# Letting GpSimd make lower parts of weights and of chunk 2's q and k, and giving a planner the measured durations of joins and upper casts

## The chip, the core and the metric

The kernel runs on one core of one Trainium2 chip. Its engines are TensorE (PE, matmuls; PEld is its weight load), VectorE (DVE), ScalarE (ACT), GpSimd (POOL) and SyncE (SP, which issues most transfers). The metric is the time on the device of one execution, in microseconds, as the median of several runs; lower is better. In this kernel about 0.2% (1.2 us) is what such a measurement tells from no change.

## The reference

Attention with a sliding window and sink columns, then a two-layer network with a leaky activation:

```python
# q, k, v: batch 4, heads 8, length 768, head size 64; window 128, sinks 4
scores = scale * np.matmul(q, k.transpose(0, 1, 3, 2))
scores = np.where(is_sink | in_window, scores, -1e9)
a = np.exp(scores - max(scores)); a = a / (sum(a) + 1e-9)
x = np.matmul(a, v)                      # as 3072 x 512
h = x @ w_in                             # 512 x 2048
g = np.maximum(h, 0) + alpha * np.minimum(h, 0)
out = g @ w_out                          # 2048 x 512
```

All inputs are float32 but the weights, which arrive as float64.

## The kernel before

**Tiling.** The 3072 rows are 12 chunks of 256 rows (c = 0 to 11, three for each batch). The 2048 hidden columns are 16 blocks of 128 (f = 0 to 15); block f holds 128 columns of w_in and 128 rows of w_out, as two halves of 512 columns each (half 0 is w_in's, half 1 w_out's). Every product of the network is made of three matmuls in a 19-bit format, high x high, high x low and low x high, where the lower part of a number is the number less its rounded upper part.

**Weights.** `convert_weights` (line 425) turns block f from float64 to these two parts in four steps over 1024 columns: an upper cast (line 436, on DVE or ACT) into the tile `zeros`, a join (line 441, DVE) into the tile `joined`, the high part (line 454, mostly ACT) and the low part (line 457, DVE, one subtraction over both halves). `zeros` and `joined` exist once, so the join of the next block waits for the low part of this one. All 16 blocks are converted between 7 and 106 us; `gemm1` (line 987) needs half 0 of a block, `gemm2` (lines 1043 to 1046) half 1.

**Attention.** From chunk 2 on, for each of 8 heads, `prep_head` (line 618) makes the high parts of k and q on ACT (lines 629, 630) and their low parts on DVE (lines 631, 633); `unit` (line 639) makes a score tile on PE (lines 668, 669) in one of two PSUM banks "s"; `soften` (line 676) adds the mask and takes the row minimum on DVE (line 683), which frees the bank, and the exponential on ACT (line 689); `finish_head` (line 693) makes 1/sum on DVE (lines 720, 721), the weighted window on DVE (line 732) and the sink columns on POOL (line 736).

**Network.** For each chunk and block, 12 matmuls of `gemm1`, the activation in three steps (ACT 996, DVE 998, ACT 1002), its low part (line 1005, on DVE, or on POOL for chunks below `ALONE`), and 6 matmuls of `gemm2`. Two neighbouring chunks may share a block: then the 12 matmuls of `gemm1` move 512 columns instead of twice 12 that move 256. `SHARED` says how many blocks chunk c shares with chunk c + 1.

**Order.** A planner (`Plan`, line 92) gets every operation with an engine, a cost in us, what it reads and writes, and for some an `other` engine with its own cost. `draw` (line 168) places them in order of time on each engine, by rank, and an operation goes to its other engine where it could start over 0.3 us sooner there. Operations with `locks` on DVE and on POOL are placed so that no two of them overlap: while one of them runs on POOL, DVE is given only operations without that mark. The order so found is fixed for each engine's queue; at run time, an engine waits at the head of its queue for what the operation needs. So a wrong cost changes no result, but puts an operation ahead of others that would have been ready.

Of the kernel before, what the change touches and what calls it, by code (L numbers as in the profile page):

```python
# [50 lines left out]
OVER = 1  # L51
# [7 lines left out]
AHEAD = 4  # L59
HALVED = 0  # L60
BUSY = 6
ALONE = 3
FIRST = 4
SHARED = {3: 3, 4: min(5, 6), **{c: 6 for c in range(5, 11)}}
EXP_LOW = 2.0 ** -15
EXP_HIGH = 122880.0
WIDEST = 2.0 ** 100
# [288 lines left out]
def program(ctx, tc, qk, pairs, vp, vq, vs, w, par, out):  # L356
# [68 lines left out]
    def convert_weights(f):  # L425
        raw, fin, first = raws[f], Block(None), None
        fins[f] = fin
        parts = ((0,), (1,)) if f < HALVED else ((0, 1),)
        for halves in parts:
            n = len(halves) * DM  # L430
            cols = slice(halves[0] * DM, halves[0] * DM + n)
            keys = lambda v, halves=halves: [(v, i) for i in halves]

            def upper(engine, cols=cols):
                to = zeros.at[:, cols].bitcast(F16).rearrange("p (x s) -> p x s", s=2)[:, :, 1]
                (nc.scalar.copy if engine == "ACT" else nc.vector.tensor_copy)(to, raw.at[:, cols].bitcast(BF16).rearrange("p x (w s) -> p x w s", s=2)[:, :, 1, 0])
            ways = [("DVE", 0.03 + 0.73e-3 * n, lambda upper=upper: upper("DVE")), ("ACT", 0.1 + 1.1e-3 * n, lambda upper=upper: upper("ACT"))]
            mine = ways.pop(f >= BUSY)
            o = op(*mine, reads=keys(raw), writes=keys(zeros), other=ways[0], locks=True)
            first = first or o  # L440
            op("DVE", 0.06 + 1.19e-3 * n, lambda cols=cols: nc.vector.scalar_tensor_tensor(
                joined.at[:, cols], raw.at[:, cols, 0], 13, zeros.at[:, cols], op0=ALU.logical_shift_right, op1=ALU.bitwise_or),
               reads=keys(raw) + keys(zeros), writes=keys(joined), locks=True)
        for halves in parts:
            a, b = halves[0], halves[-1] + 1
            keys = lambda v, halves=halves: [(v, i) for i in halves]
            n = (b - a) * DM
            wf = lambda a=a, b=b: joined.at.bitcast(F32).rearrange("p (i x) -> p i x", i=2)[:, a:b]

            def high_part(engine, a=a, b=b, wf=wf):  # L450
                if fin.at is None:
                    fin.tile = const.tile([P, 2, 2, DM], F32R, tag=f"w{f}", name=f"w{f}")
                    fin.at = [fin.tile[:, i] for i in range(2)]
                (nc.scalar.copy if engine == "ACT" else nc.vector.tensor_copy)(fin.tile[:, a:b, 0], wf())
            op("ACT", cast(n), lambda high_part=high_part: high_part("ACT"), reads=keys(joined), writes=[(fin, (i, 0)) for i in halves] + ([raw] if a == 0 else []),
               other=("DVE", dve(n, True), lambda high_part=high_part: high_part("DVE")))
            op("DVE", dve(n), lambda a=a, b=b, wf=wf: nc.vector.tensor_tensor(
                fin.tile[:, a:b, 1], wf(), fin.tile[:, a:b, 0].bitcast(F32), ALU.subtract),
               reads=keys(joined) + [(fin, (i, 0)) for i in halves], writes=[(fin, (i, 1)) for i in halves], locks=True)
        return first  # L460

    def weigh(f):
# [155 lines left out]
    def prep_head(c, h):  # L618
        st = stage.pop((c, h))
        if c in SPLIT:  # L620
            r = slice(h % 2 * D, (h % 2 + 1) * D)
            prep[c, h] = (st, r)
            return
        kq = val("kq")
        qh, ql = [lambda s=s: kq.at[:, s] for s in (slice(2 * KG, 2 * KG + QC), slice(2 * KG + QC, 2 * KG + 2 * QC))]
        n = 0 if c % CPB else P
        ks = lambda: kq.at[:, :2 * KG].rearrange("p (y x) -> p y x", y=2)[:, :, :KX]
        q_raw, k_raw = lambda: st.at[:, KC:], lambda: st.at[:, :KC].rearrange("p (y x) -> p y x", y=2)[:, :, n // 2:]
        op("ACT", cast(KC - n), lambda: nc.scalar.copy(ks()[:, :, n // 2:], k_raw()), reads=[st], writes=[(kq, "k")])  # L629
        op("ACT", cast(QC), lambda: nc.scalar.copy(qh(), q_raw()), reads=[st], writes=[(kq, "q")])  # L630
        op("DVE", dve(KC - n), lambda: nc.vector.tensor_tensor(ks()[D:, :, n // 2:], k_raw()[D:], ks()[D:, :, n // 2:].bitcast(F32), ALU.subtract),  # L631
           reads=[st], writes=[(kq, "k")], locks=True)
        op("DVE", dve(QC), lambda: nc.vector.tensor_tensor(ql(), q_raw(), qh().bitcast(F32), ALU.subtract),
           reads=[st, (kq, "q")], writes=[(kq, "l")], locks=True)
        prep[c, h] = (kq, qh, ql, ks)

    softened = []
# [55 lines left out]
    def finish_head(c, h):  # L693
        pt, nm, sm = ptile_.pop((c, h)), nms[c], sums[c]
        sk = sink[c]
        if h == H - 1:
            op("DVE", 0.1, lambda: nc.vector.tensor_tensor(fm, fm, nm.at.rearrange("p h u -> p (h u)"), ALU.max),
               reads=[nm], writes=[known("fm")])
        if c in SPLIT:
            op("POOL", 0.17, lambda: nc.gpsimd.tensor_copy(sk.at[:, :, h], pt.at[:, :, P:P + NS]), reads=[pt], writes=[(sk, h)])  # L700
            tp = bank(c, h, "pa")
            for u in range(2):
                o = 2 * u * P
                both = u > 0 or c % CPB > 0

                def turn(u=u, o=o, both=both):
                    if both:
                        nc.tensor.transpose(tp.at[:, o:o + P], pt.at[:, u, 0:P], ident)
                    nc.tensor.transpose(tp.at[:, o + P:o + 2 * P], pt.at[:, u, P + NS:], ident)
                op("PE", (1 + both) * TURN, turn, reads=[(pt, u), known("ident")], writes=[tp], tail=T_TAIL)  # L710
            o = P if c % CPB == 0 else 0
            lends = c == 0 and h >= 4
            t = val("v" if lends else "comb")
            turned_ = (lambda: t.at.rearrange("p a h d -> p (a h d)")) if lends else (lambda: t.at[:, o:])
            op("ACT", cast(4 * P - o, True), lambda: nc.scalar.copy(turned_(), tp.at[:, o:]), reads=[tp], writes=[t],
               other=("DVE", dve(4 * P - o), lambda: nc.vector.tensor_copy(turned_(), tp.at[:, o:])) if c == 0 else None)
            wt.setdefault((c, h // 2), []).append((t, lambda cols: turned_()[:, cols.start - o:cols.stop - o]))
            return
        ri = val("ri")
        op("DVE", 0.15, lambda: nc.vector.tensor_scalar(ri.at[:, :2], sm.at[:, h], 1e-9, None, op0=ALU.add), reads=[(sm, (h, 0)), (sm, (h, 1))], writes=[ri], locks=True)  # L720
        op("DVE", 0.08, lambda: nc.vector.reciprocal(ri.at[:, :2], ri.at[:, :2]), writes=[ri])  # L721
        if h % 2 == 0:
            comb[c, h // 2] = val("comb")
        cb = comb[c, h // 2]
        view = lambda: cb.at.rearrange("p (j u x) -> p j u x", j=2, u=2)[:, h % 2]
        for u in range(2):
            if u == 0 and c % CPB == 0:
                op("DVE", 0.2, lambda: nc.vector.tensor_scalar(view()[:, 0], pt.at[:, 0, P + NS:], ri.at[:, 0:1], None, op0=ALU.mult),
                   reads=[(pt, 0), ri], writes=[(cb, (h % 2, 0))], locks=True)
                continue  # L730
            jk = val("jk")
            op("DVE", 0.28, lambda u=u, jk=jk: nc.vector.tensor_tensor_reduce(  # L732
                out=view()[:, u], in0=pt.at[:, u, 0:P], in1=pt.at[:, u, P + NS:], scale=ri.at[:, u:u + 1], scalar=0.0,
                op0=ALU.add, op1=ALU.max, accum_out=jk.at[:, u:u + 1]),
                reads=[(pt, u), ri], writes=[(cb, (h % 2, u)), jk])
        op("POOL", 0.2, lambda: nc.gpsimd.tensor_tensor(  # L736
            sk.at[:, :, h], pt.at[:, :, P:P + NS], ri.at[:, :2].unsqueeze(2).broadcast_to([P, 2, NS]), ALU.mult),
            reads=[pt, ri], writes=[(sk, h)])
        if c >= PAIRED and h % 2:
            swap(c, h // 2)  # L740
# [425 lines left out]
    groups += [[(0, f), (1, f)] for f in range(LEAD, NF)]  # L1166
    groups += [[(1, f), (1, f + 1)] for f in range(FORE, LEAD, 2)]
    work = [[] for _ in range(2 * NF)]
    for at_, steps in ((0, spread(attention(1), OVER)), (2 * NF - LATE, spread([st for some in attention(2) for st in some or [None]] + [None] * 4, LATE))):
        for n, todo in enumerate(steps):  # L1170
            work[at_ + n] += todo
    pend = []
# [262 lines left out]
```

## Time and profile before

| | |
|---|---|
| median of three runs | 619.73 us (619.46 to 619.85) |
| the profiled execution | 619.43 us, of which span 617.6 us |
| PE / PEld busy | 609.1 us (99%) / 541.2 us (88%) |
| DVE / ACT / POOL busy | 484.2 (78%) / 379.4 (61%) / 44.6 us (7%) |
| granted TensorE clock, mean | 0.999 |

A row of a timeline is: start, duration, engine, line, operation, output and inputs, shapes, count, and in brackets how long the engine had been idle before and what ended that. A matmul's duration is that from its first column to its last result; the next one may start before it ends. Line numbers are those of the kernel before.

### The profile page before, as it was taken

What the parts mean: (1) busy time and instruction counts of PE and PEld (TensorE: products, weight loads), DVE (VectorE), ACT (ScalarE), POOL (GpSimd) and SP (SyncE); (2) the same over time, 40 slices, a digit from 0 to 9 for tenths busy, and PEclk for the clock granted to TensorE, in tenths of its full rate; (3) what the DMA queues carried; (4) which work ended last, traced back from release to release, by engine and by line L of the source; (5) the groups of instructions that cost most, each with busy time, mean ns of one, the idle gap of its engine ahead of it and who ended that gap; (6) DMA issues with size and microseconds to landing.
All of it is one profiled execution on the core that took longest, in us unless ns stands there. A gap on an engine that the chain in (4) does not pass through costs nothing. (4 is left out here: it accounts for less than half of the span.)

```text
span 617.6 us, 13165 instructions
## 1 busy us (share of the span) xinstructions
PE 609.1 (99%) x4607; PEld 541.2 (88%) x4607; DVE 484.2 (78%) x1587; ACT 379.4 (61%) x984; POOL 44.6 (7%) x124
## 2 busy tenths in 40 slices
PE   8999999999999999999999999999999999999996
PEld 4688878999999989988988988998998998998895
DVE  7999999969899889689689789769769969842341
ACT  6998887557568466465466457456466556369232
POOL 3120120001000000011000000010000000000000
PEclk9999999999999999999999999999999999999999
DMA  8968662445545444444444444534434443300011
GB/s 329 338 211 272 221 225 65 145 147 153 162 123 184 127 144 152 124 123 138 128 132 136 129 133 131 154 99 141 138 112 138 124 130 100 120 36 0 1 36 37
DMA packets 68280, 85.52 MB, mean 138 GB/s; under 512 B 10864, under 2 KB 49264, under 8 KB 68208
## 3 DMA queue, kind: packets, MB, share of 16 engines
q1 hardware_dynamic: 64512, 71.65, 36.9%
q10 hardware_dynamic: 3696, 12.98, 5.9%
q8 instruction: 37, 0.61, 0.4%
q14 instruction: 35, 0.29, 0.2%
HBM read 66.49 MB, written 18.12 MB: 137 GB/s over the span
## 5 line engine op out<-in xcount | busy, mean ns | idle before, releaser
L987 PE MATMUL bank<-xh,w 128*128 128x256 f32 (+1 forms) x1104 | 261.1, 317 | 0.0
L987 PEld LDWEIGHTS bank<-xh,w 128*128 128x128 f32 x1104 | 188.2, 191 | 12.2 <-issue 0.7
L987 PE MATMUL bank<-xl,w 128*128 128x256 f32 (+1 forms) x552 | 174.4, 316 | 0.0
L996 ACT ACTIVATE g<-bank,param 128x256 f32<-128x256 f32 (+1 forms) x138 | 76.8, 557 | 113.5 <-PE bank L987 112.5
L1045 PE MATMUL bank<-w,gh 128*128 128x512 f32 x380 | 145.3, 382 | 0.0
L1046 PE MATMUL bank<-w,gh 128*128 128x512 f32 x380 | 144.0, 379 | 0.0
L1043 PE MATMUL bank<-w,gl 128*128 128x512 f32 x380 | 113.3, 380 | 0.0
L998 DVE TENSOR_TENSOR g<-bank,g 128x256 f32<-128x256 f32 (+1 forms) x138 | 71.9, 524 | 49.4 <-ACT g L996 48.5
L987 PEld LDWEIGHTS bank<-xl,w 128*128 128x128 f32 x552 | 105.2, 191 | 5.7
L689 ACT ACTIVATE pt<-pt,nm 128x260 f32<-128x260 f32 (+1 forms) x192 | 93.4, 488 | 7.6 <-DVE nm L683 7.5
L1002 ACT CAST gh<-g 128x256 fp32r<-128x256 f32 (+1 forms) x138 | 66.8, 487 | 49.1 <-DVE g L998 48.4
L683 DVE CUSTOM_DVE_ANT_0 pt<-bank,masks 128x260 f32<-128x260 f32 (+1 forms) x192 | 71.9, 402 | 18.6 <-PE bank L669 16.7
L1005 DVE TENSOR_TENSOR gl<-g,gh 128x256 fp32r<-128x256 f32 (+1 forms) x130 | 68.0, 526 | 22.4 <-ACT gh L1002 20.3
L1045 PEld LDWEIGHTS bank<-w,gh 128*128 128x128 f32 x380 | 71.9, 189 | 9.1 <-issue 0.2
L1043 PEld LDWEIGHTS bank<-w,gl 128*128 128x128 f32 x380 | 70.8, 189 | 9.6
L1046 PEld LDWEIGHTS bank<-w,gh 128*128 128x128 f32 x380 | 71.9, 189 | 8.3
L629 ACT CAST kq<-stage 128x392 fp32r<-128x392 f32 (+1 forms) x80 | 38.7, 483 | 38.7 <-PE bank L669 29.0
L736 POOL TENSOR_TENSOR sink<-pt,ri 128x8 f32<-128x8 f32 x80 | 20.8, 262 | 359.5 <-DVE ri L721 278.5
L732 DVE CUSTOM_DVE_ANT_0 comb<-pt,ri 128x128 f32<-128x128 f32 x136 | 44.3, 350 | 0.7
L631 DVE TENSOR_TENSOR kq<-stage,kq 64x392 fp32r<-64x392 f32 (+1 forms) x80 | 42.0, 525 | 3.1 <-ACT kq L629 0.4
L668 PE MATMUL bank<-kq 128*128 128x260 f32 (+1 forms) x160 | 40.8, 277 | 1.4 <-DVE nm L683 1.3
L669 PE MATMUL bank<-kq 128*128 128x260 f32 (+1 forms) x160 | 41.5, 274 | 0.0
(132 smaller groups left out, 676.6 us busy)
## 6 DMA issues: line engine op xcount, KB each, us to landing
stage<-qk SPq DMA_DIRECT2D x56, 324.0 KB, 2.9
wraw<-w ACTq DMA_DIRECT2D x12, 1023.5 KB, 5.1
swap<-comb SPq DMA_DIRECT2D x40, 256.0 KB, 2.3
stage<-qk SPq DMA_DIRECT2D x24, 292.0 KB, 2.8
out_dram<-ob SPq DMA_DIRECT2D x22, 256.0 KB, 2.4
v<-vq SPq DMA_DIRECT2D x28, 192.0 KB, 3.3
wa<-swap SPq DMA_DIRECT2D x40, 128.0 KB, 2.9
wraw<-w SPq DMA_DIRECT2D x4, 1023.5 KB, 9.0
```

What stands on the lines that cost most here:

```text
L631: op("DVE", dve(KC - n), lambda: nc.vector.tensor_tensor(ks()[D:, :, n // 2:], k_raw()[D:], ks()[D:, :, n // 2:].bitcast(F32), ALU.subtrac ...
L683: o = op("DVE", dve(n), lambda: nc.vector.tensor_tensor_reduce(out=pt.at[:, u, w0], in0=s.at[:, w0], in1=masks[:, i, w0], scale=-0.125, sc ...
L689: op("ACT", exp(n), lambda: nc.scalar.activation(pt.at[:, u, w0], pt.at[:, u, w0], AF.Exp, bias=nm.at[:, h, u:u + 1], scale=-1.0, accum_ou ...
L732: op("DVE", 0.28, lambda u=u, jk=jk: nc.vector.tensor_tensor_reduce(out=view()[:, u], in0=pt.at[:, u, 0:P], in1=pt.at[:, u, P + NS:], scal ...
L987: nc.tensor.matmul(h(), fin.win(part, ks), moving(name, kt), start=(kt == 0 and m == 0), stop=(kt == KT - 1 and m == 2))
L996: op("ACT", act(width, True), lambda g=g, h=h, view=view, f=f: nc.scalar.activation(view(g), h(), AF.Copy, scale=alt[:, f:f + 1]), reads=[ ...
L998: op("DVE", dve(width), lambda g=g, h=h, view=view: nc.vector.tensor_tensor(view(g), h(), view(g), ALU.max), reads=[bk], writes=keys(g))
L1002: op("ACT", cast(width), lambda g=g, gh=gh, view=view: nc.scalar.copy(view(gh), view(g)), reads=keys(g), writes=keys(gh))
L1005: on.tensor_tensor(view(gl), view(g), view(gh).bitcast(F32), ALU.subtract)
L1043: nc.tensor.matmul(o2[j].at, gl.at[:, i, js], fin.row(0), start=False, stop=(f == end))
L1045: nc.tensor.matmul(o2[j].at, gh.at[:, i, js], fin.row(0), start=(f == begin), stop=False)
L1046: nc.tensor.matmul(o2[j].at, gh.at[:, i, js], fin.row(1), start=False, stop=False)
```

## The change

The lower part of a weight block is made in two subtractions of 512 columns, one for each half, and each of them may go to POOL. The low parts of k and q may go to POOL where c < `ALONE`, which is raised from 3 to 4; since chunks 0 and 1 take another way, that is chunks 2 and 3, and the low parts of `gemm1`'s results of chunk 3 may go to POOL as well. The planner's costs of the join and of the upper cast on ACT are set to other values, larger ones from f = 7 on. The first step of 1/sum may go to ACT. The weighted window (line 732) gets the mark `locks`. Chunk 3 shares 4 blocks with chunk 4 instead of 3, chunk 4 shares 6 with chunk 5 instead of 5. The steps of chunk 2's attention are spread over the same 21 places with 3 empty ones at their end instead of 4.

```diff
-ALONE = 3
+ALONE = 4
-SHARED = {3: 3, 4: min(5, 6), **{c: 6 for c in range(5, 11)}}
+SHARED = {3: 4, 4: 6, **{c: 6 for c in range(5, 11)}}
...
-            ways = [("DVE", 0.03 + 0.73e-3 * n, ...), ("ACT", 0.1 + 1.1e-3 * n, ...)]
+            ways = [("DVE", 0.03 + 0.73e-3 * n, ...), ("ACT", 0.1 + (1.1e-3 if f < 7 else 1.4e-3) * n, ...)]
...
-            op("DVE", 0.06 + 1.19e-3 * n, lambda cols=cols: nc.vector.scalar_tensor_tensor(
+            op("DVE", 0.06 + (1.15e-3 if f < 7 else 1.25e-3 if f == 7 else 1.43e-3) * n, lambda cols=cols: nc.vector.scalar_tensor_tensor(
...
-            op("DVE", dve(n), lambda a=a, b=b, wf=wf: nc.vector.tensor_tensor(
-                fin.tile[:, a:b, 1], wf(), fin.tile[:, a:b, 0].bitcast(F32), ALU.subtract),
-               reads=keys(joined) + [(fin, (i, 0)) for i in halves], writes=[(fin, (i, 1)) for i in halves], locks=True)
+            for i in halves:
+                def low_part(on, i=i, a=a, wf=wf):
+                    on.tensor_tensor(fin.tile[:, i, 1], wf()[:, i - a], fin.tile[:, i, 0].bitcast(F32), ALU.subtract)
+                op("DVE", dve(DM), lambda low_part=low_part: low_part(nc.vector), reads=[(joined, i), (fin, (i, 0))], writes=[(fin, (i, 1))], locks=True,
+                   other=("POOL", pool2(DM), lambda low_part=low_part: low_part(nc.gpsimd)))
...
+        low_k = lambda on: on.tensor_tensor(ks()[D:, :, n // 2:], k_raw()[D:], ks()[D:, :, n // 2:].bitcast(F32), ALU.subtract)
+        op("DVE", dve(KC - n), lambda: low_k(nc.vector), reads=[st], writes=[(kq, "k")], locks=True,
+           other=("POOL", pool2(KC - n), lambda: low_k(nc.gpsimd)) if c < ALONE else None)
+        low_q = lambda on: on.tensor_tensor(ql(), q_raw(), qh().bitcast(F32), ALU.subtract)
+        op("DVE", dve(QC), lambda: low_q(nc.vector), reads=[st, (kq, "q")], writes=[(kq, "l")], locks=True,
+           other=("POOL", pool2(QC), lambda: low_q(nc.gpsimd)) if c < ALONE else None)
...
         op("DVE", 0.15, lambda: nc.vector.tensor_scalar(ri.at[:, :2], sm.at[:, h], 1e-9, None, op0=ALU.add), reads=..., writes=[ri], locks=True,
+           other=("ACT", 0.2, lambda: nc.scalar.activation(ri.at[:, :2], sm.at[:, h], AF.Copy, bias=1e-9)))
...
                 op0=ALU.add, op1=ALU.max, accum_out=jk.at[:, u:u + 1]),
-                reads=[(pt, u), ri], writes=[(cb, (h % 2, u)), jk])
+                reads=[(pt, u), ri], writes=[(cb, (h % 2, u)), jk], locks=True)
...
-    ... (2 * NF - LATE, spread([st for some in attention(2) for st in some or [None]] + [None] * 4, LATE))):
+    ... (2 * NF - LATE, spread([st for some in attention(2) for st in some or [None]] + [None] * 3, LATE))):
```

## Rows read from the trace of the kernel before

**Rows 1.** The page's busy times, each with its share and instructions.

```profile
PE 609.1 (99%) x4607; PEld 541.2 (88%) x4607; DVE 484.2 (78%) x1587; ACT 379.4 (61%) x984; POOL 44.6 (7%) x124
```

**Rows 2.** Stretches of the span: length, busy time of each engine, clock, DMA.

```profile
0.00:24.00 24.00, 22.13 (x138) 12.26 (x139) 19.91 (x74) 17.25 (x54) 6.82 (x24) 1.00 0.90 333
24.00:60.00 36.00, 35.99 (x266) 29.90 (x265) 33.97 (x77) 34.09 (x78) 5.78 (x11) 1.00 0.75 251
60.00:84.00 24.00, 24.00 (x119) 21.06 (x118) 22.43 (x42) 20.19 (x35) 3.98 (x4) 1.00 0.69 247
84.00:106.00 22.00, 20.61 (x99) 16.92 (x98) 21.07 (x47) 17.93 (x32) 2.42 (x4) 1.00 0.32 108
106.00:540.00 434.00, 433.87 (x3470) 395.66 (x3469) 361.97 (x1288) 249.93 (x705) 25.64 (x81) 1.00 0.44 135
```

**Rows 3.** Waits over the span: who waited for whom, total, times, longest.

```profile
PEld bank L668 <- DVE nm L683: 2.3, 4, 1.0
PE bank L668 <- DVE nm L683: 1.3, 3, 0.6
```

**Rows 4.** Timeline of PE around the first of these waits.

```profile
84.09 0.59 PE L1043 MATMUL bank<-w,gl 128*128 128x512 f32 x2
85.25 0.38 PE L668 MATMUL bank<-kq 128*128 128x260 f32 x1 [0.57 <-DVE nm L683]
```

**Rows 5.** Timeline of DVE ahead of the same wait.

```profile
82.74 1.52 DVE L441 SCALAR_TENSOR_TENSOR wa<-wraw,wa 128x1024 int32<-128x1024 int32 x1
84.18 0.68 DVE L998 TENSOR_TENSOR g<-bank,g 128x512 f32<-128x512 f32 x1
84.78 0.42 DVE L683 CUSTOM_DVE_ANT_0 pt<-bank,masks 128x260 f32<-128x260 f32 x1
```

**Rows 6.** DVE's groups from 60 to 106 us: count, busy, mean ns, idle before.

```profile
L441 DVE SCALAR_TENSOR_TENSOR wa<-wraw,wa 128x1024 int32<-128x1024 int32 x8 | 12.4, 1546 | 0.9 <-ACT wa L436 0.8
L457 DVE TENSOR_TENSOR w<-wa,w 128x1024 fp32r<-128x1024 f32 x8 | 9.8, 1223 | 1.2 <-ACT w L454 1.0
L998 DVE TENSOR_TENSOR g<-bank,g 128x512 f32<-128x512 f32 x8 | 5.5, 682 | 0.0
L683 DVE CUSTOM_DVE_ANT_0 pt<-bank,masks 128x260 f32<-128x260 f32 x12 | 5.0, 420 | 0.0
L1005 DVE TENSOR_TENSOR gl<-g,gh 128x512 fp32r<-128x512 f32 x5 | 3.4, 687 | 0.1
L631 DVE TENSOR_TENSOR kq<-stage,kq 64x392 fp32r<-64x392 f32 x6 | 3.4, 564 | 0.2
L732 DVE CUSTOM_DVE_ANT_0 comb<-pt,ri 128x128 f32<-128x128 f32 x6 | 3.0, 520 | 0.0
L633 DVE TENSOR_TENSOR kq<-stage,kq 128x256 fp32r<-128x256 f32 x6 | 2.5, 422 | 0.2
```

**Rows 7.** ACT's upper casts and high parts from 60 to 106 us.

```profile
L436 ACT CAST wa<-wraw 128x1024 f16<-128x1024 bf16 x7 | 10.9, 1560 | 0.0
L454 ACT CAST w<-wa 128x1024 fp32r<-128x1024 f32 x8 | 8.4, 1045 | 4.4 <-DVE wa L441 4.4
```

**Rows 8.** Timeline of POOL: a low part of 512 columns.

```profile
79.59 1.75 POOL L1005 TENSOR_TENSOR gl<-g,gh 128x512 fp32r<-128x512 f32 x1 [10.10 <-ACT gh L1002]
```

**Rows 9.** Timeline of DVE at the same time.

```profile
78.97 1.23 DVE L457 TENSOR_TENSOR w<-wa,w 128x1024 fp32r<-128x1024 f32 x1
80.11 0.42 DVE L683 CUSTOM_DVE_ANT_0 pt<-bank,masks 128x260 f32<-128x260 f32 x1
80.65 0.84 DVE L732 CUSTOM_DVE_ANT_0 comb<-pt,ri 128x128 f32<-128x128 f32 x1
81.42 0.34 DVE L732 CUSTOM_DVE_ANT_0 comb<-pt,ri 128x128 f32<-128x128 f32 x1
```

**Rows 10.** Timeline of DVE: the low part of block f = 5.

```profile
47.61 1.23 DVE L457 TENSOR_TENSOR w<-wa,w 128x1024 fp32r<-128x1024 f32 x1
```

**Rows 11.** Timeline of PE: the first matmul with block f = 5.

```profile
49.92 0.27 PE L987 MATMUL bank<-xh,w 128*128 128x256 f32 x1
```

**Rows 12.** Timeline of PE: the second matmul of one unshared block, and of the next.

```profile
115.07 0.28 PE L987 MATMUL bank<-xl,w 128*128 128x256 f32 x1
116.41 0.28 PE L987 MATMUL bank<-xl,w 128*128 128x256 f32 x1
```

More of the change, by code (lines that the diff above doesn't have):

```diff
@@ L436, in upper @@
                 (nc.scalar.copy if engine == "ACT" else nc.vector.tensor_copy)(to, raw.at[:, cols].bitcast(BF16).rearrange("p x (w s) -> p x w s", s=2)[:, :, 1, 0])
-            ways = [("DVE", 0.03 + 0.73e-3 * n, lambda upper=upper: upper("DVE")), ("ACT", 0.1 + 1.1e-3 * n, lambda upper=upper: upper("ACT"))]
+            ways = [("DVE", 0.03 + 0.73e-3 * n, lambda upper=upper: upper("DVE")), ("ACT", 0.1 + (1.1e-3 if f < 7 else 1.4e-3) * n, lambda upper=upper: upper("ACT"))]
             mine = ways.pop(f >= BUSY)
@@ L630, in prep_head @@
         op("ACT", cast(QC), lambda: nc.scalar.copy(qh(), q_raw()), reads=[st], writes=[(kq, "q")])
[L631 to L634, printed above, removed]
+        low_k = lambda on: on.tensor_tensor(ks()[D:, :, n // 2:], k_raw()[D:], ks()[D:, :, n // 2:].bitcast(F32), ALU.subtract)
[4 more added lines that the diff above has]
+           other=("POOL", pool2(QC), lambda: low_q(nc.gpsimd)) if c < ALONE else None)
         prep[c, h] = (kq, qh, ql, ks)
@@ L719, in finish_head @@
         ri = val("ri")
-        op("DVE", 0.15, lambda: nc.vector.tensor_scalar(ri.at[:, :2], sm.at[:, h], 1e-9, None, op0=ALU.add), reads=[(sm, (h, 0)), (sm, (h, 1))], writes=[ri], locks=True)
+        op("DVE", 0.15, lambda: nc.vector.tensor_scalar(ri.at[:, :2], sm.at[:, h], 1e-9, None, op0=ALU.add), reads=[(sm, (h, 0)), (sm, (h, 1))], writes=[ri], locks=True,
+           other=("ACT", 0.2, lambda: nc.scalar.activation(ri.at[:, :2], sm.at[:, h], AF.Copy, bias=1e-9)))
         op("DVE", 0.08, lambda: nc.vector.reciprocal(ri.at[:, :2], ri.at[:, :2]), writes=[ri])
@@ L1168, in program @@
     work = [[] for _ in range(2 * NF)]
-    for at_, steps in ((0, spread(attention(1), OVER)), (2 * NF - LATE, spread([st for some in attention(2) for st in some or [None]] + [None] * 4, LATE))):
+    for at_, steps in ((0, spread(attention(1), OVER)), (2 * NF - LATE, spread([st for some in attention(2) for st in some or [None]] + [None] * 3, LATE))):
         for n, todo in enumerate(steps):
```

## The prediction

> **What bounds the kernel now.** First the busy times: PE is busy 99% of the span, and the change neither adds nor removes products but for how wide some of them are [rows 1]. So the first question is where PE loses time at all. The stretches answer it: from 106 to 540 us PE is busy 433.87 of 434 us, from 24 to 60 us 35.99 of 36, from 60 to 84 all of it; in the stretch from 84 to 106 us it lacks 1.39 of 22 us, and in the first 24 us 1.87 [rows 2]. The opening waits for the first loads and the first chunk's attention; the stretch behind 84 us is the last place where DVE is nearly full, 21.07 of 22 us after 22.43 of 24 [rows 2]. The waits tell the same: four times the score matmul of line 668 waits for DVE's line 683, which frees one of two PSUM banks, 2.3 us at the weight load and 1.3 us as idle PE [rows 3]. In the timeline the last of two matmuls that start 0.215 us apart begins at 84.31, could have been followed at 84.52, and the score matmul begins at 85.25: 0.73 us lost, of which the row shows 0.57 as idle because the last matmul is still draining [rows 4]. With that 0.16 us for each, the idle 1.3 us in three waits is 1.8 us of PE; 2.3 us is the bound from above. I take **2.0 us**: that is all there is to win in this stretch.
>
> Why is DVE late there? Ahead of that wait it ran a join of 1.52 us, then line 998, then line 683 [rows 5]. The planner charged that join 0.06 + 1.19e-3 x 1024 = 1.28 us. The eight joins from 60 to 106 us took 1.546 us on average [rows 6], so DVE falls behind its plan by 8 x 0.27 = 2.1 us over the stretch; ACT's seven upper casts took 1.56 us [rows 7] against 1.23 planned, 2.3 us more. PE's queue was laid out for a DVE two microseconds faster than it is, and PE waits two microseconds.
>
> **The change, part by part.**
>
> *Costs.* With the new ones a join from f = 8 on is charged 0.06 + 1.43e-3 x 1024 = 1.52 us and an upper cast 0.1 + 1.4e-3 x 1024 = 1.53, within 0.03 of the rows [rows 6, 7]. This takes no work away. It lets the planner put gemm matmuls, which are ready, ahead of a score whose bank isn't free, and so turns waits into order. PE has such work as long as blocks of weights are ready.
>
> *Halves of a block.* DVE starts its next operation a little before the last one's end: behind 512 columns after 0.60 (84.18 to 84.78 [rows 5]), behind a low part of 1024 after 1.14 (78.97 to 80.11 [rows 9]). Two halves of 512, whose nearest row is line 1005 with 687 ns [rows 6], so cost 2 x 0.61 on DVE: 0.08 us more for a block, 1.3 us over 16, beside PE's work. On POOL a half costs: the low part of 512 columns has a span of 1.75 us [rows 8], but it begins while DVE's line 457 still runs, to 80.11, and ends at 81.34; 1.23 us of it is its own. During it line 683, which reads PSUM, took its usual 0.42, while line 732, which reads two tiles in SBUF, took 0.84 instead of 0.34 and ended right behind POOL [rows 9]. So POOL works beside DVE only where DVE has something that doesn't read two SBUF tiles; the planner's mark models this, and now covers line 732.
>
> How many halves can go? From 60 to 106 us DVE's two-tile work is 12.4 + 9.8 + 3.4 + 3.4 + 2.5, and line 732 without its delay 6 x 0.34 = 2.0: 33.5 us [rows 6]. Three low parts on POOL hold the same port for about 3.7 us more, together 37.2 of 46 us. Each half that moves adds 1.23 - 0.61 = 0.62 us to that and takes 0.61 us from DVE. Port time is full at (46 - 37.2) / 0.62 = 14 of the 16 halves; I expect 4 to 8, which frees 2.4 to 4.9 us of DVE, plus the 1.0 us that line 732 lost behind POOL [rows 9]. That is more than the 2.1 us by which it runs late.
>
> The Trainium skill ("SBUF — State Buffer", section on SBUF's two separate sides) calls the port pair that VectorE and GpSimd share an exclusive lock held for a whole instruction, also against VectorE operations with two SBUF inputs. The trace agrees: the 0.84 us row ends with POOL's [rows 8, 9]. By that rule each moved half is a loss of port time and never a gain; the sum then is the second rival's.
>
> *Low parts of k and q.* On DVE 564 and 422 ns [rows 6]. POOL's price for 392 columns isn't in the trace: not under DVE's 0.56, not over the 1.23 of 512 columns; by columns 0.94. Same exchange, smaller; scores wait for them, so the planner will move few. Chunk 3's `gemm1` low parts likewise; behind 106 us DVE has slack (361.97 of 434 [rows 2]), so nothing is to be gained there.
>
> *Cover.* A low half on POOL is 0.62 us later, two of them 1.25, and `joined` is held as much longer. Block 5 has its low part at 48.84 and is used at 49.92 [rows 10, 11]: 1.08 us of cover. Half 0 alone is needed there, so one half fits, two in a row are at the edge. POOL's own queue: the sink columns of line 736 stand behind the halves, needed only when the chunk's heads are done. At nothing, covered by that.
>
> *1/sum on ACT* stands ahead of line 732 alone; no row shows ACT on two columns. Between 0 and the 0.16 us that it would take off DVE each; taken as 0.
>
> *Sharing.* Two more shared blocks. Twelve matmuls over 256 columns take 116.41 - 115.07 = 1.34 us [rows 12], so a block for two chunks 2.68; shared, 12 x 0.215 = 2.58 [rows 4]. **0.2 us** less for both. The attention of chunks 4 and 5 starts one block earlier, where PE is full and DVE has slack.
>
> *Chunk 2's steps* come up to one place later. That moves scores away from the busiest stretch by at most one block; bounds -0.2 and +0.2, taken as 0.
>
> *A new order* everywhere up to about 250 us: where there are hardly any waits now (0.13 us of 434 lack [rows 2]), a new one can only add some. The four waits average 2.0 / 4 = 0.5 us; I charge one small wait, 0.2 us, bounds 0 and 1.
>
> **Sum**, against the profiled execution (619.43, span 617.6 and 1.83 around it; 0.3 below the median): three of the four waits, 1.5, and 0.2 for sharing, less 0.2: 1.5 us. 619.43 - 1.5 = 617.9; by the median 619.73 - 1.5 = **618.2 us**, 0.24% less.
>
> **Rivals.**
>
> *A wait takes the place of the one removed.* DVE is relieved, but the join, the high part and the low part of a block still go one after the other through one `joined`: 1.55 + 1.05 + 1.22 [rows 6, 7]. Scores then wait for other things just as long. For it: DVE stays over 90% busy. Against it: PE waits for nothing but line 683 there [rows 3]. It gives 619.73 - 0.2 and a little new waiting: 619.5, between 618.6 and 620.6.
>
> *The shared port becomes the bound: slower.* If the planner hands over nearly all halves in the stretch, all joins, casts of low parts and windows queue behind POOL. It decides from 14 halves on 60 to 106 us, or from two in a row for a block with 1.08 us of cover. Price: both halves of a block on POOL hold `joined` 2 x 0.62 = 1.25 us longer; if a third of the eight blocks pass that on to PE, 3.3 us, less the 1.5 us of the forecast: about 621.5. Against it: the planner keeps marked operations apart and charges 0.3 us for the other engine.
>
> *It does more than it says.* All four waits go, and the opening, where DVE is busy 19.91 of 24 us [rows 2] and PE lacks 1.87, gains one subtraction of a block, 1.2 us: 619.73 - 2.0 - 0.2 - 1.0 = 616.5.
>
> **Chances.** Forecast 0.50 (own range 617.3 to 618.9), moved wait 0.25, slower 0.15, more 0.10. About 0.2%, 1.24 us, can be told from no change, so faster means under 618.49 and slower over 620.97. Faster: 0.38 of the forecast's 0.50, 0.02 of the moved wait, the 0.10: 0.50. Slower: 0.12 of its 0.15, 0.03 of the moved wait: 0.15. Same: 0.35. The range leaves out half of the last case and the far end of the slower one: 616.7 to 621.0.
>
> **What would show it.** Right: the row of line 668 waiting for the soften step falls from 2.3 us to under 0.8, PE lacks under 0.5 us in the stretch from 84 to 106 us, four to eight low halves stand on POOL there, and line 732 is back to about 0.35 us each. Wrong: PE's weight loads wait for low halves or for scores' inputs on POOL, DVE's two-tile operations show twice their durations, or the opening's first gemm matmul moves by over half a microsecond, which I hold for unmoved.

## The result, and the profile after

The changed kernel takes 624.15 us (median of six, 623.68 to 624.66) against 619.59 (619.0 to 619.85) for the kernel before on the same chip: ratio 1.0080, 95% interval 1.0070 to 1.0091; the medians are 4.6 us apart, the ratio gives 5.0. Forecast were 618.2 us and a range up to 621.0. The profiled span is 622.6 us against 617.6.

The stretches of the span of the changed kernel (length; busy us and count of PE, PEld, DVE, ACT, POOL; clock; DMA), to be laid beside [rows 2]:

```profile
0.00:24.00 24.00, 21.35 (x128) 11.95 (x129) 19.98 (x74) 15.54 (x50) 8.50 (x26) 1.00 0.89 329
24.00:60.00 36.00, 35.12 (x259) 27.28 (x258) 32.73 (x73) 30.66 (x72) 12.54 (x15) 1.00 0.66 226
60.00:84.00 24.00, 23.57 (x115) 20.31 (x114) 23.44 (x41) 17.75 (x32) 5.48 (x4) 1.00 0.81 278
84.00:106.00 22.00, 22.00 (x109) 19.43 (x109) 21.20 (x47) 19.45 (x36) 5.59 (x7) 1.00 0.32 102
106.00:140.00 34.00, 33.01 (x312) 29.42 (x311) 27.16 (x91) 19.09 (x54) 7.59 (x12) 1.00 0.49 152
```

The last of these stretches in the kernel before:

```profile
106.00:140.00 34.00, 34.00 (x328) 31.02 (x327) 26.34 (x96) 18.48 (x51) 1.88 (x4) 1.00 0.47 149
```

From 84 to 106 us, the stretch on which the prediction dwelt, PE now lacks nothing, where it lacked 1.39 us. But the wait that was to go is still there, at other places. Waits of PE and PEld over the span of the changed kernel (line 672 is 668 before, 687 is 683):

```profile
PEld bank L672 <- DVE nm L687: 2.3, 4, 1.0
PE bank L672 <- DVE nm L687: 1.0, 2, 0.6
PE bank L791 <- DVE ri L756: 0.6, 1, 0.6
PE bank L876 <- DVE ob L762: 0.4, 1, 0.4
```

The weight load waits for the soften step 2.3 us in four waits, as before; PE stands for it at 78.7 and at 117.6 us. From 106 to 140 us PE lacks 0.99 us, where it lacked nothing. The larger loss is ahead of all that, from 0 to 60 us, where POOL's busy time rose from 12.6 to 21.0 us.

Equal times of two kernels are not equal work. So for the tables below each matmul of the trace is counted with the usual distance from one of its kind to the next, and the time is read at which PE has done as much; matmuls that only fill idle time (line 1228 before) aren't counted. By this count the changed kernel lags the one before by 1.7 us when 15 us of products are done, 4.2 at 40, 4.9 at 70, 2.5 at 90, 4.1 at 115 and 5.1 at 250; behind that it stays at 5.1. The start of the first shared block shows the same 4.2 us in plain rows. Timeline of PE, kernel before:

```profile
56.96 0.38 PE L987 MATMUL bank<-xh,w 128*128 128x512 f32 x1
```

and changed kernel:

```profile
60.75 0.59 PE L1048 MATMUL bank<-w,gl 128*128 128x512 f32 x2
61.18 0.38 PE L992 MATMUL bank<-xh,w 128*128 128x512 f32 x1
```

What happens in the opening, in the timeline of POOL:

```profile
17.39 0.19 POOL L704 COPY sink<-pt 128x8 f32<-128x8 f32 x1 [0.29 <-ACT pt L693]
17.54 2.50 POOL L459 TENSOR_TENSOR w<-wa,w 128x512 fp32r<-128x512 f32 x2
25.32 1.28 POOL L459 TENSOR_TENSOR w<-wa,w 128x512 fp32r<-128x512 f32 x1 [5.28 <-ACT w L454]
```

and of DVE beside it:

```profile
17.61 1.29 DVE L771 CAST ts<-sink 128x128 fp32r<-128x128 f32 x1 [0.57 <-POOL sink L704]
18.93 1.25 DVE L773 TENSOR_TENSOR ts<-sink,ts 128x128 fp32r<-128x128 f32 x1
```

The two low halves of block 0 (line 459 now) begin at once behind POOL's sink copy, at 17.54. DVE's sink steps, which were waiting for that same copy, are issued 0.07 us later and each stands for one half's 1.25 us instead of some 0.25. They are on the path to the first chunk's attention: PE's waits for lines 756 and 762 above end at 20.3 and 21.2 us. The groups of DVE from 14 to 60 us (count, busy, mean ns, idle before) show the same for four such steps, in the changed kernel:

```profile
L900 DVE TENSOR_TENSOR xl<-ob,xh 128x512 fp32r<-128x512 f32 x4 | 4.3, 1076 | 0.0
L773 DVE TENSOR_TENSOR ts<-sink,ts 128x128 fp32r<-128x128 f32 x3 | 2.3, 750 | 0.1
L771 DVE CAST ts<-sink 128x128 fp32r<-128x128 f32 x3 | 1.8, 587 | 1.4 <-POOL sink L704 1.4
L756 DVE TENSOR_SCALAR ri<-sm 128x8 f32<-128x8 f32 x3 | 1.6, 520 | 0.0
```

Ten of the 32 low halves went to POOL: six of blocks 0 to 5, all between 17 and 51 us, and four from 77 to 109 us. The low parts of k and q that moved do the same further on. POOL and DVE ahead of PE's wait at 117.6 us (line 737 is the window, 732 before):

```profile
114.55 0.76 POOL L633 TENSOR_TENSOR kq<-stage,kq 64x264 fp32r<-64x264 f32 x1 [1.71 <-ACT kq L631]
115.40 0.73 POOL L636 TENSOR_TENSOR kq<-stage,kq 128x256 fp32r<-128x256 f32 x1
```

```profile
114.63 0.84 DVE L737 CUSTOM_DVE_ANT_0 comb<-pt,ri 128x128 f32<-128x128 f32 x1
115.40 0.88 DVE L737 CUSTOM_DVE_ANT_0 comb<-pt,ri 128x128 f32<-128x128 f32 x1
```

```profile
117.56 0.38 PE L672 MATMUL bank<-kq 128*128 128x260 f32 x1 [0.56 <-DVE nm L687]
```

Two windows of usually 0.34 us are 1.0 us late together, and the soften step queued behind them frees PE's bank late.

### The profile page after: what moved, and what is told of

It reads as the page before. It is cut to its first block, busy times and chain, and to the rows that moved or that the text cites. A ratio compares the mean times of both kernels' runs of the same rounds, so it can differ in the third digit from the quotient of the medians.

```text
span 622.6 us, 13142 instructions
## 1 busy us (share of the span) xinstructions
PE 611.7 (98%) x4586; PEld 541.7 (87%) x4586; DVE 487.1 (78%) x1582; ACT 375.0 (60%) x980; POOL 64.0 (10%) x141
## 5 line engine op out<-in xcount | busy, mean ns | idle before, releaser
L992 PEld LDWEIGHTS bank<-xh,w 128*128 128x128 f32 x1088 | 186.1, 191 | 13.9 <-DVE g L1003 1.7
L992 PEld LDWEIGHTS bank<-xl,w 128*128 128x128 f32 x544 | 103.7, 191 | 5.7
L1010 DVE TENSOR_TENSOR gl<-g,gh 128x256 fp32r<-128x256 f32 (+1 forms) x129 | 69.7, 542 | 22.6 <-ACT gh L1007 20.9
L633 DVE TENSOR_TENSOR kq<-stage,kq 64x392 fp32r<-64x392 f32 (+1 forms) x74 | 39.6, 535 | 2.4
```

Of the source, the lines that this page charges most:

```text
L992: nc.tensor.matmul(h(), fin.win(part, ks), moving(name, kt), start=(kt == 0 and m == 0), stop=(kt == KT - 1 and m == 2))
L1010: on.tensor_tensor(view(gl), view(g), view(gh).bitcast(F32), ALU.subtract)
```

## The experiments

**Theory.** The planner keeps the marked steps of DVE and POOL apart in its own time, but nothing on the chip does. POOL's queue is short and starts a moved step as soon as its input lands, ahead of the DVE step that the planner placed first; then DVE stands for 1.25 us with everything behind it. **Rivals:** the port time as such is too much; the new order of the queues loses, whoever does the halves; the new costs lose; sharing loses.

The runs were taken in four sets, each on one chip, with the kernel before at 619.45 us (the runs named e1 to e4), 619.40 (f), 618.92 (g and h) and 619.55 (i). So sets are compared by the ratio, and an expectation in us, written for 619.5, is 0.6 us too high for g and h. In the text, "by the ratio" means the ratio times 619.5.

**e1_swap, e2_held: the order is kept, one thing is changed.** Both keep the planner's order of the changed kernel; e1_swap issues the six early halves on DVE at the same place in it.

```diff
 e1_swap
-            self.emit(o.ways[e][1])
+            self.emit(o.ways["DVE" if getattr(o, "early", False) else e][1])   # early: low halves with f < LEAD
 e2_held
+            ...
+            if e == "POOL" and o.engine == "DVE" and held_by:
+                self.tc.add_manual_dep(ins[0], held_by[-1].name, ...Sync...)
+            if e == "DVE" and o.locks:
+                held_by[:] = ins[-1:]
```

> The changed kernel with every queue in the same order, but the six low halves of blocks 0 to 5 that went to GpSimd are issued on VectorE, at the place that the order gives them. Theory (GpSimd takes the shared port ahead of VectorE's sink and window steps): the VectorE steps that took 1.2 to 1.8 us instead of 0.2 to 0.7 are back to their usual times; 5.2 us of blocking goes and 6 x 0.6 = 3.7 us of subtraction comes, so some 1.5 us of the 4.2 us lost before 58 us comes back: 622.6, between 621.5 and 623.2. Rival (the new order of the queues is itself the loss): within 0.5 us of the changed kernel's 624.15, or slower by VectorE's extra work, up to 626.

Measured: 621.93 us, ratio 1.0042 (1.0028 to 1.0056). 2.2 us back, within the theory's range. The lag at 40 us of products falls from 4.2 to 2.2.

> The changed kernel with every queue in the same order, but each step that was moved from VectorE to GpSimd waits for the VectorE step that the planner placed ahead of it and that uses the same port. Theory (on the chip nothing makes GpSimd keep the planned turn; it starts as soon as its input lands and takes the port first): most of the loss before 58 us goes, 2 to 3 us of 4.2, so 621.2 to 622.2. Rival (two halves of 1.23 us each hold the port too long wherever they stand): no change within 0.5 us of 624.15, since the same port time is used.

Measured: **619.67 us**, ratio 1.0006 (0.9996 to 1.0015): the same as the kernel before. 4.5 of the 4.6 us come back, more than expected, with the same steps on POOL. The lag at 250 us of products falls by as much, from 5.1 to 0.5. Timeline of POOL in e2_held:

```profile
18.41 2.69 POOL L467 TENSOR_TENSOR w<-wa,w 128x512 fp32r<-128x512 f32 x2 [0.75 <-DVE ri L764]
```

and its groups of DVE from 14 to 60 us, in the same order as above:

```profile
L908 DVE TENSOR_TENSOR xl<-ob,xh 128x512 fp32r<-128x512 f32 x4 | 3.5, 870 | 0.0
L781 DVE TENSOR_TENSOR ts<-sink,ts 128x128 fp32r<-128x128 f32 x3 | 0.9, 293 | 0.1
L779 DVE CAST ts<-sink 128x128 fp32r<-128x128 f32 x3 | 0.7, 232 | 1.4 <-POOL sink L712 1.4
L764 DVE TENSOR_SCALAR ri<-sm 128x8 f32<-128x8 f32 x3 | 0.5, 165 | 0.0
```

POOL waits 0.75 us for line 764 (756 above) and begins 0.87 us later; the four groups are 0.8 + 1.4 + 1.1 + 1.1 = 4.4 us shorter. The first shared block starts at 58.17 us, 3.0 before that of the changed kernel. The wait for the soften step (line 680 for 695 here) is half of what it was, and none of it shows as idle PE:

```profile
PEld bank L680 <- DVE nm L695: 1.1, 3, 0.5
```

Together this settles the main cause: not that POOL does the halves, but when it takes its turn. Collisions aren't all gone. Line 709 (701 above), two SBUF tiles of 16 columns without the mark, took 0.16 us in the changed kernel and now stands behind a held half. Timeline of DVE in e2_held:

```profile
48.16 1.19 DVE L709 TENSOR_TENSOR fm<-fm,nm 128x16 f32<-128x16 f32 x1
```

**g2_hold_early, g1_share_unheld: where holding counts, and whether in other orders too.**

```diff
 g2_hold_early (on e2_held)
-            if e == "POOL" and o.engine == "DVE" and held_by:
+            if e == "POOL" and getattr(o, "early", False) and held_by:
```

> The changed kernel in its own order, where only the six low halves of blocks 0 to 5 that went to GpSimd are held, none of the later moved steps. Theory (the early halves take the port ahead of the first chunks' sink and window steps and so cost most): 3 us of the 4.5 come back, 621.0 to 621.5, with the opening as in e2_held up to 50 us. Rival (the loss is spread evenly over all moved steps, six of some twenty): about 622.8.

Measured: 621.23 us beside 618.92 for the kernel before, ratio 1.0035 (1.0023 to 1.0048). The opening is nearly back (lag 1.6 at 40), but of the whole only 2.3 us by the medians, 2.8 by the ratio. In us the time stands in the theory's range, but the ratio makes it 621.7 against 619.5, between theory and rival. The rest belongs to the other moved steps, nearly all of it behind 50 us: the lag exceeds e2_held's by 0.4 at 40 us of products and 0.9 at 70. At 250 it is 2.8, but the profiled execution is the slowest of the six, 1.1 us over their median, so some 1.1 us of that isn't typical.

> f1_share with the holding taken out again and every queue in the same order: the changed kernel with sharing as before. Theory (holding is worth some 4.5 us in any order that has many moved halves, and sharing some 2): 622.0 to 622.5. Rival (holding was worth so much only in the changed kernel's own order): under 620.5.

Measured: 621.61 us beside 618.92, ratio 1.0043 (1.0026 to 1.0059). By the ratio that is 622.2 against 619.5, as the theory had it. Against f1_share (0.9972, below), which differs in the holding alone, 0.7% or 4.4 us. So holding is worth as much in an order of another sharing, and the rival is out.

**e4_late, f6_late_held: no early halves.** Both planned anew.

```diff
-                   other=("POOL", pool2(DM), lambda low_part=low_part: low_part(nc.gpsimd)))
+                   other=("POOL", pool2(DM), lambda low_part=low_part: low_part(nc.gpsimd)) if f >= LEAD else None)
```

> The changed kernel, planned anew, where only the low halves of blocks 6 to 15 may go to GpSimd. Theory (the early halves on GpSimd are the 4.2 us lost before 58 us): that loss goes and the gain between 84 and 106 us stays, 619 to 621. Rival (costs or the other edits make the opening slow): 622.5 or more, with the loss before 58 us still there.

Measured: 621.12 us, ratio 1.0024 (1.0014 to 1.0034). The opening's loss goes (lag 0.8 at 40), the total is just over the expected range: 2.4 us at 250. f6_late_held shows that this belongs to later moved steps that aren't held.

> The changed kernel where only low halves of blocks 6 to 15 may go to GpSimd, and the moved steps are held. Theory (e4_late loses by unheld turns as the changed kernel does, only fewer of them): 0.5 to 1.5 us less than e4_late, 619.6 to 620.6, not clearly better than e2_held, since early halves do no harm once held. Rival (early halves cost even when held): under 619.2.

Measured: 618.75 us, ratio 0.9990 (0.9980 to 0.9999): better than the theory's range and under its rival's bound, which said that early halves cost even when held. Against e4_late, which differs in the holding alone, it is 0.34% or 2.1 us less. It is 0.16% below e2_held's ratio, with overlapping intervals, so that early halves cost is a hint and no more.

**e3_costs, f5_before_held_costs, i1_costs_all_held: the costs alone.** The kernel before with the new costs of join and upper cast; then also with the window's mark and held low parts; then with POOL's line 531 (a lower part of the sink rows of v, which always was POOL's) held as well.

```diff
 i1_costs_all_held (on f5_before_held_costs)
-            if e == "POOL" and o.engine == "DVE" and held_by:
+            if e == "POOL" and (o.engine == "DVE" or o.cost > 1) and held_by:
```

> The kernel before with the new planner costs of the join and of the upper cast on ScalarE alone; nothing goes to GpSimd that didn't. Theory (costs cure the waits for the soften step between 60 and 106 us and leave the opening alone): 1 to 2 us less than the kernel before, 617.6 to 618.6, and the opening as before. Rival (any new order loses in the opening): 621 or more.

Measured: 619.15 us, ratio 1.0001 (0.9991 to 1.0010). No gain, though the stretch did what the theory said: from 70 to 90 us of products the lag falls from 3.0 to 0.9, with no half on POOL. In the changed kernel it falls from 4.9 to 2.5. So that gain needs no half on POOL. That the costs alone make it isn't shown: PE had lost 2.2 us just ahead, a time in which DVE can catch up, and f4_before_held wins 1.2 us there (from 0.4 to -0.8) with the old costs. The losses of e3_costs are 0.9 us before 40 and 2.2 near 57 us. The timelines of POOL, DVE and PE in e3_costs there:

```profile
55.49 1.97 POOL L531 TENSOR_TENSOR vs<-ob,vs 64x512 fp32r<-64x512 f32 x1 [8.81 <-ACT vs L529]
```

```profile
56.25 1.75 DVE L895 TENSOR_TENSOR xl<-ob,xh 128x512 fp32r<-128x512 f32 x1
```

```profile
58.06 0.38 PE L987 MATMUL bank<-xl,w 128*128 128x256 f32 x1 [1.29 <-DVE xl L895]
```

An old step of POOL does here what the moved ones do in the changed kernel: it waits at the port behind the join, gets it at about 56.2, and DVE's line 895, for which PE waits, ends after POOL.

> As f4_before_held, with the new costs of join and upper cast as well. Theory (the costs cure waits for the soften step, holding removes port collisions): 617.5 to 618.8. Rival (the costs make a new order that waits elsewhere, as in e3_costs, where 2.2 us were lost near 58 us): 619 or more.

Measured: 619.04 us, ratio 0.9993 (0.9983 to 1.0003): the rival's. Line 531 isn't held in it, and the same 2.2 us are lost.

> f5_before_held_costs with every queue in the same order, where the four GpSimd steps of line 531 are held as well. Theory (GpSimd takes the port ahead of VectorE's line 895, which the planner placed first, and TensorE waits for that): the wait of 1.3 us for line 895 near 57 us goes, 1.3 to 2.2 us less than f5_before_held_costs, 616.9 to 617.8. Rival (the order made by the new costs loses there whatever GpSimd does): 618.7 to 619.3.

Measured: 619.09 us, ratio 0.9993 (0.9983 to 1.0002): a miss. The timelines of DVE and PE in i1_costs_all_held say why:

```profile
56.63 0.68 DVE L903 TENSOR_TENSOR xl<-ob,xh 128x512 fp32r<-128x512 f32 x1
57.82 2.08 DVE L465 TENSOR_TENSOR w<-wa,w 128x1024 fp32r<-128x1024 f32 x1 [0.52 <-ACT w L462]
59.83 0.74 DVE L1006 TENSOR_TENSOR g<-bank,g 128x256 f32<-128x256 f32 x2
```

```profile
57.36 0.38 PE L995 MATMUL bank<-xl,w 128*128 128x256 f32 x1 [0.25 <-DVE xl L903]
60.29 0.48 PE L995 MATMUL bank<-xh,w 128*128 128x512 f32 x1 [1.44 <-DVE g L1006]
```

Line 903 (895 before) is at its usual 0.68 us and PE's wait for it falls from 1.30 us in f5_before_held_costs to 0.25. But the POOL step, now behind it (57.54 to 58.82 us), stands beside the low part of a block, which takes 2.08 us instead of 1.22, and line 1006 (998 before), queued behind that, makes PE wait 1.44 us instead of 0.36. The collision was moved on by one step and its price with it. So a held step helped here only where the DVE step that it meets next isn't waited for.

**f1_share, h1_late_share: sharing as before.**

```diff
-SHARED = {3: 4, 4: 6, **{c: 6 for c in range(5, 11)}}
+SHARED = {3: 3, 4: min(5, 6), **{c: 6 for c in range(5, 11)}}
```

> The changed kernel with the moved steps held as in e2_held, but chunk 3 shares 3 blocks and chunk 4 five, as before the change. Theory (two more shared blocks give 0.2 us, and starting chunks 4 and 5 a block earlier puts scores where VectorE is fuller, which costs the 0.85 us seen near 131 us or the 0.8 us near 253 us): 0.2 us more for the blocks and 0.8 to 1.6 less for those waits, 618.3 to 619.1. Rival (sharing is clean): 619.9, and the waits near 131 and 253 us stand.

Measured: **617.72 us**, ratio 0.9972 (0.9961 to 0.9983), better than expected. e2_held loses 0.7 us near 253 us, which f1_share doesn't. PE and DVE in e2_held:

```profile
252.94 0.28 PE L1000 MATMUL bank<-xh,w 128*128 128x256 f32 x1
253.76 0.38 PE L1000 MATMUL bank<-xh,w 128*128 128x256 f32 x1 [0.55 <-DVE g L1011]
```

```profile
252.37 0.42 DVE L845 TENSOR_TENSOR comb<-comb,tri 64x256 f32<-64x256 f32 x1 [1.81 <-DMA comb<-swap]
252.83 0.42 DVE L848 TENSOR_TENSOR comb<-comb,tri 64x256 f32<-64x256 f32 x1
253.28 0.42 DVE L1011 TENSOR_TENSOR g<-bank,g 128x256 f32<-128x256 f32 x1
```

DVE stands 1.81 us for a transfer of the attention that was placed one block earlier, with the activation that frees PE's bank queued behind it. The wait near 131 us stands in both; the expectation was wrong on that. The rest of the gap between the two, 1.0 us, lies behind the last matmul: 5.4 us from its start to the end of the span in e2_held, 4.4 in f1_share. The same holds against the kernel before, where it is 5.5: of the 1.7 us by which f1_share is shorter, the lag shows 0.4.

> f6_late_held with sharing as before. Theory (two more shared blocks cost 0.8 us near 253 us through the earlier start of chunks 4 and 5, in this order too): 617.6 to 618.0. Rival (that wait belongs to e2_held's order alone): 618.7 to 619.0.

Measured: **616.50 us** beside 618.92, ratio 0.9960 (0.9946 to 0.9975): 2.4 us under the kernel before, better than the theory's range, and clearly better than both kernels. Of these 2.4 us the lag shows 1.3; the rest lies behind the last matmul (4.4 us against 5.5). By the count f6_late_held falls back 1.4 us between 230 and 250 us of products, and h1_late_share doesn't.

**f4_before_held: what holding is worth without moved work.**

```diff
-                reads=[(pt, u), ri], writes=[(cb, (h % 2, u)), jk])
+                reads=[(pt, u), ri], writes=[(cb, (h % 2, u)), jk], locks=True)
 and the holding of e2_held
```

> The kernel before, where the low parts of the network's results that go to GpSimd wait for the VectorE step planned ahead of them, and the weighted window has the mark that keeps it away from GpSimd's steps; nothing else. Theory (GpSimd taking its turn early costs this kernel too, but only in the eight low parts it has there): 0.3 to 1.2 us less, 618.2 to 619.2, and the windows of 0.84 and 0.95 us are back to 0.35. Rival (holding GpSimd only helps where many halves were moved): 619.4 to 619.8.

Measured: 618.12 us, ratio 0.9980 (0.9971 to 0.9990), just under the theory's range. But only 0.4 of these 1.3 us stand in the lag at 250; 0.9 lie behind the last matmul (4.7 us against 5.5), where holding has no part that a row shows. So the total doesn't prove the theory; the windows do. The window's group from 60 to 106 us, to be laid beside its row of [rows 6]:

```profile
L740 DVE CUSTOM_DVE_ANT_0 comb<-pt,ri 128x128 f32<-128x128 f32 x6 | 2.0, 339 | 0.0
```

339 ns instead of 520, and the opening as before (lag 0.1 at 40).

**h2_old_early_costs, i2_best: the costs of the early blocks.** f1_share and h1_late_share with the join's old cost for blocks 0 to 6; i2_best also holds line 531.

```diff
-(1.15e-3 if f < 7 else 1.25e-3 if f == 7 else 1.43e-3)
+(1.19e-3 if f < 7 else 1.25e-3 if f == 7 else 1.43e-3)
```

> f1_share with the planner's old, larger cost of the join for blocks 0 to 6 and the new ones from block 7 on. Theory (the 1.2 us that every kernel with the new costs loses before 48 us comes from the order that the smaller early cost makes; f4_before_held, with old costs, loses none): 616.3 to 617.0. Rival (the loss comes with the halves or another edit): 617.5 to 618.5.

Measured: 617.13 us beside 618.92, ratio 0.9971 (0.9960 to 0.9982): no better than f1_share and just over the theory's range; by the ratio (617.7 against 619.5) it is in the rival's. The opening does gain 1.1 us (lag 0.3 at 40 instead of 1.3), and the order behind 100 us gives 1.6 us of it back (lag -2.2 there, -0.6 at 115), 1.0 us of it in one wait of PE for a transfer (line 961 for sinkT, at 127.5 us). The step is right, its worth for the total isn't.

> h1_late_share with the join's old cost for blocks 0 to 6 and with line 531 held too. Theory (each of the two is worth 0.3 to 1.2 us in its own place): 615.3 to 616.3. Rival (a new order takes with another wait what it gives): 616.5 to 617.5, no better than h1_late_share.

Measured: **616.51 us** beside 619.55, ratio 0.9949 (0.9933 to 0.9966): the fastest, though not told apart from h1_late_share; its opening lags 1.2 us at 40 all the same. The time is 0.2 us over the theory's range and at the edge of the rival's, and its ratio is only 0.0011 under h1_late_share's, so a worth of the two steps isn't shown.

The lag behind the kernel before, in us, when PE has done so many us of products:

| kernel | 15 | 40 | 70 | 90 | 115 | 250 |
|---|---|---|---|---|---|---|
| changed kernel | 1.7 | 4.2 | 4.9 | 2.5 | 4.1 | 5.1 |
| e1_swap | 1.4 | 2.2 | 3.0 | 0.6 | 2.1 | 2.7 |
| e2_held | 0.6 | 1.2 | 1.5 | -0.9 | -0.1 | 0.5 |
| g2_hold_early | 0.6 | 1.6 | 2.4 | -0.1 | 1.5 | 3.4 |
| e4_late | 0.5 | 0.8 | 1.4 | -0.3 | 1.1 | 2.4 |
| e3_costs | 0.5 | 0.9 | 3.0 | 0.9 | 0.6 | 0.8 |
| f4_before_held | 0.1 | 0.1 | 0.4 | -0.8 | -0.4 | -0.4 |
| f1_share | 0.8 | 1.3 | 1.7 | -0.8 | 0.1 | -0.4 |
| h1_late_share | 0.9 | 1.2 | 1.3 | -1.1 | -1.4 | -1.3 |

The kernel before is there at 26.7, 53.3, 83.3, 105.7, 133.1 and 274.6 us. The lag doesn't hold what lies behind the last matmul: from its start to the end of the span 5.4 to 5.7 us in the kernel before, the changed kernel, e1_swap, e2_held, g2_hold_early, e4_late and f6_late_held, and 4.3 to 4.7 in all others. All kernels with the new sharing are in the first group, but so is the kernel before, with the old sharing; so what sets it is open. A difference of totals between the two groups has some 1.1 us of it. The pairs that show what holding is worth (changed kernel and e2_held, g1_share_unheld and f1_share, e4_late and f6_late_held) lie within one group each.

## Why the prediction was wrong

*The waits behind 60 us: right in size for that stretch, but they came back.* 2.0 us to win and 1.5 expected; the changed kernel wins 2.4 between 70 and 90 us of products and loses 1.6 again by 115. The sign put for being right, line 668's wait under 0.8 us, didn't come: it is 2.3 as before. With the turns held it is 1.1 us at the weight load, none of it as idle PE, and most of the gain stays (lag 1.5 at 70, -0.1 at 115). So the diagnosis fits that DVE is late there by its plan; relief of DVE by halves wasn't needed (e3_costs and f4_before_held win 2.1 and 1.2 there without it), and what each of costs, mark and holding gives isn't told apart.

*"The planner keeps marked operations apart": the step that failed.* It stood as the argument against the slower rival, and it is true of the plan only. The kernel before showed the contrary: in [rows 8, 9] POOL's low part is queued while line 457 runs, which has the mark too, and takes the port before line 732. So does the opening, for two marked steps. POOL and DVE, kernel before:

```profile
31.65 0.73 POOL L1005 TENSOR_TENSOR gl<-g,gh 128x256 fp32r<-128x256 f32 x1
```

```profile
31.75 0.71 DVE L766 CAST ts<-sink 128x128 fp32r<-128x128 f32 x1
```

The prediction used [rows 8, 9] for a price and read their cause as a missing mark; that no wait ties POOL's turn to DVE's was there to be read. In its sum this stood as nothing for the port and 0.2 us for a new order. e2_held puts the step at 4.5 us, the whole result. Of that, g2_hold_early gives 2.3 to 2.8 us to the six early halves, the rest to the other moved steps.

*"POOL works beside DVE only where DVE has something that doesn't read two SBUF tiles": too narrow.* The cast of line 766 (771 in the changed kernel) and line 756 read one tile; they took 0.71 and 1.24 us behind POOL instead of 0.23 and 0.17.

*Low parts of k and q: taken as worth nothing.* Two of the eight that moved make the windows of line 737 late and cost PE some 0.7 us at 117.6 us (0.56 as idle); with them held that wait is gone.

*The opening held for unmoved.* It lost 4.2 us by 40 us of products. The prediction counted halves and port time from 60 to 106 us, where it saw the wait; six of the ten halves that moved are of the first blocks, where the port count wasn't made. The sentence that a gemm matmul moving there by half a microsecond would be the sign of error was the right one to write.

*The slower rival: its outcome, not its mechanism.* It gave 621.5 us by a port that is full from 14 halves on, and a chance of 0.15. Three halves moved in that stretch, and with the same halves held the time is that of the kernel before. So the point from which it decides was wrong: one half is enough, if it begins ahead of a DVE step on the path. Its other condition, two halves of a block in a row, did come about for block 0, but PE waits there for the sink steps and not for the block. The effect was given to the wrong quantity, the sum of the port time, where the order of the turns decides. The rule of the Trainium skill on the exclusive lock ("SBUF — State Buffer", the section on two separate sides) agrees with the rows: the sink steps at 17.61 and 18.93 us stand for 1.29 and 1.25 us, a half each.

*Sharing: 0.2 us less forecast.* Undoing it took 0.9 us off e2_held's lag and lowered the ratio from 1.0006 to 0.9972, some 2 us, of which 1.0 lies behind the last matmul; whether that belongs to sharing is open. The matmuls are cheaper as worked out, but the start of two chunks' attention a block earlier isn't free: DVE's slack there is an average, and its queue stood 1.81 us for a transfer.

*One small wait for a new order: mis-sized.* With the moved steps held, the new order still lags 1.2 us at 40. In f1_share's order about 1 us of that goes with the old costs of the early joins (h2_old_early_costs); in h1_late_share's it doesn't (i2_best). So it differs from order to order.

*Still open:* the 1.1 us behind the last matmul, what the costs are worth alone, and whether early halves cost anything once held. That a held step of POOL merely shifts its collision, as in i1_costs_all_held, wasn't tried elsewhere.

## What to carry to other kernels

A plan that keeps two engines apart in its own time must tie them on the chip too, by a wait of the moved step for the one planned ahead of it; here that wait was worth 4.5 of 624 us. It doesn't help every time: in i1_costs_all_held the price only moved on. Put the measured costs in first, alone, and see what is left to move: in e3_costs the wait that the change was for went without any half on POOL, though a new order lost as much elsewhere (ratio 1.0001). And count what a moved step can block everywhere it may stand, not only in the stretch that it is meant to help.

## What the runs showed of the hardware

A GpSimd subtraction of 512 float32 columns took 1.25 to 1.32 us where it had the port at once (2.50 us for two at 17.54 us, 1.27 at 30.80, 1.32 at 33.15 in the changed kernel). Its span in the trace was 1.78 us at 49.01 us in the changed kernel and 1.97 in e3_costs, where it began while a VectorE step was still running. So a long POOL row here is a sign of a collision and not of slow work. A VectorE step caught behind it took the whole remainder of that time, however short it is itself: 1.24 us, at 33.26 us in the changed kernel, for the one of line 756 with 128 x 8 elements that else took 0.17. The single-input cast of line 771 was held up as much (1.29 us at 17.61 us, else 0.22 to 0.25) as the two-input step behind it (1.25 us).
